# One weight load of 8 MB cut into four strided loads at the start of a streaming attention kernel

## The chip, the cores and the metric

The kernel runs on one core of a Trainium2 chip. The metric is the device time of one launch in microseconds (us). It was run three times for that: 1309.45, 1309.56 and 1309.97 us, with a median of 1309.56 us. One further execution was taken with the profiler. Its lines are those quoted below.

## The reference

Four tokens `x` (4 x 512) go through two branches whose outputs are mixed by a gate.

```
q = (x @ wq) as 32 heads of 128             # wq: 512 x 4096 f32, 8 MB
scores = q . k_cache / sqrt(128)            # k_cache: 4 x 32 x 4096 x 128 f32, 256 MB
a = softmax(scores) . v_cache @ wo          # v_cache: the same size; wo: 4096 x 512
b = (gelu(x @ w_gate) * (x @ w_up)) @ w_down   # 512 x 1792 twice, 1792 x 512
g = sigmoid(sum(x * gate_w))
out = g * a + (1 - g) * b
```

Every byte of the two caches is read once, and little is computed with each. Of the 565 MB that are read, `wq` is 8 MB.

## The kernel before

**Tiling.** The caches are cut into 32 tiles each, one for a token (4) and a group of four heads (8). A tile is 8 MB: 128 partitions with 64 KB each. One large SBUF buffer, `big`, holds two K tiles, which overlap by a quarter, and one V tile. Before the first K tile has been used, the place of the V tile holds `wq`.

**Order.** The kernel records its steps in a `Plan`. Each step has an engine, a lane (a semaphore of its own) and the ranges that it reads and writes; the plan works out from these who waits for whom. `play` then emits the steps: the waits, the instruction, and an increment of the lane's semaphore by the lane's unit, which is 16 for a load. All loads are issued from one queue, that of SyncE (SP), in the order in which they are recorded: `load` records one, `load_kv` a tile of a cache, `load_f`, `load_d` and `load_w` the other weights.

**The start.** The opening steps are played inside a critical section, which the other engines leave after SP has issued them. They are four loads: `wq` (lane `q`), `x` (lane `x`, 4 rows of 2 KB), `gate_w` (lane `g`, sent to 4 partitions) and the first K tile (lane `k`). `wq` is viewed as 128 rows of 64 KB, one for each partition: partition p holds four rows of the weight matrix. Then the constants and masks are made, `x` is transposed (L307), `q_project` (L325) multiplies it by `wq` in 64 short matmuls, and VectorE puts the result in the form that all later tiles use. `load_f` reuses the place of `wq`, so its loads wait for `q_project`.

**The steady part.** For each tile VectorE multiplies K by q (L379) and sums over the head dimension (L385), ScalarE takes the exponential, and TensorE multiplies by V (L411). The next K tile is loaded once the shared quarter of the present one is done with, and the next V tile once TensorE is done with the last. At the end `w_down` and `wo` follow, and the output of 8 KB is stored (L603).

In the text, a *mover* is one of the 16 DMA engines of the core, a *row* is the 64 KB of one partition, which a mover carries as one packet, and *landing* is the arrival of a transfer's last semaphore increment.

Of the kernel before, what the change touches and what calls it, by code (L numbers as in the profile page):

```python
# [19 lines left out]
class Plan:  # L20
# [18 lines left out]
    def add(self, engine, emit, reads=(), writes=(), lane=None, unit=1):  # L39
        lane = lane or engine  # L40
        self.units[lane] = unit
        row = self.by_lane.setdefault(lane, [])
        step = Step(lane, engine, emit, self.turn if engine in self.loops else None)
        step.at = len(row)
        need = {}
        for accesses, writing in ((reads, False), (writes, True)):
            for name, lo, hi in accesses:
                for other, a, b, wrote in self.past.get(name, ()):
                    if a < hi and lo < b and (wrote or writing):
                        if other.lane == engine and engine == "pe":  # L50
                            continue
                        if other.lane == engine and not wrote:
                            continue
                        need[other.lane] = max(need.get(other.lane, -1), other.at)
        seen = self.seen[engine]
        for l, n in sorted(need.items(), key=lambda x: -len(self.by_lane[x[0]])):
            if seen.get(l, -1) >= n:
                continue
            other = self.by_lane[l][n]
            other.asked = True  # L60
            step.waits[l] = n
            seen[l] = n
            for k, v in self.knew[other].items():
                seen[k] = max(seen.get(k, -1), v)
        step.waits = {l: n for l, n in step.waits.items()
                      if not any(self.knew[self.by_lane[m][k]].get(l, -1) >= n for m, k in step.waits.items() if m != l)}
        self.knew[step] = dict(seen)
        self.knew[step][lane] = step.at
        if row and lane == engine:
            for k, v in self.knew[row[-1]].items():  # L70
                if k != lane:
                    self.knew[step][k] = max(self.knew[step].get(k, -1), v)
        for accesses, writing in ((reads, False), (writes, True)):
            for name, lo, hi in accesses:
                old = self.past.get(name, [])
                if writing:
                    old = [x for x in old if not (lo <= x[1] and x[2] <= hi)]
                self.past[name] = old + [(step, lo, hi, writing)]
        row.append(step)
        self.steps.append(step)  # L80
        return step
# [14 lines left out]
    def wants(self, step):  # L96
        return {l: self.by_lane[l][n].value for l, n in step.waits.items()}

    def play(self, steps, wants=None):
        for s in steps:  # L100
            e = self.engines[s.engine]
            for l, v in sorted((wants(s) if wants else self.wants(s)).items()):
                e.wait_ge(self.sems[l], v)
            last = s.emit()
            if s.asked:
                last.then_inc(self.sems[s.lane], self.units[s.lane])

    def loop(self, engine):
        steps = [s for s in self.steps if s.engine == engine and s.turn is not None]
# [23 lines left out]
def tile_gated_mix(tc: tile.TileContext, x, kc, vc, wq, wo, w_gate, w_up, w_down, gate_w, out):  # L133
    nc = tc.nc
    P = 128
    B, H, S, D = kc.shape
    DM = x.shape[2]
    F = w_gate.shape[1]
    KC = DM // P
# [27 lines left out]
    def sb(pool, name, shape):  # L167
        sizes[name] = math.prod(shape[1:])
        return pool(name, [P] + list(shape[1:]), F32).ap()[:shape[0]]
# [37 lines left out]
    q = sb(ps, "q", [P, B, D])  # L207
# [6 lines left out]
    Q0, F0, F1, W0, D0 = VA, VA, VA + KC * F, VA, VA + TW // 2  # L214
# [4 lines left out]
    def place(a, n):  # L219
        return big[:, a:a + n]  # L220

    def z(a, n):
        return ("big", a, a + n)
# [14 lines left out]
    plan = Plan(nc)  # L238
    add = plan.add
# [14 lines left out]
    def load(dst, src, writes, lane):  # L254
        return add("sp", lambda: nc.sync.dma_start(dst, src), (), writes, lane=lane, unit=16)  # L255
# [28 lines left out]
            else:  # L284
                load(place(a, m), src[:, e0 * DM:e1 * DM], [z(a, m)], lane)

    load(place(Q0, KC * H * D), wq.rearrange("(p c) n -> p (c n)", c=KC), [z(Q0, KC * H * D)], "q")
    load(x_sb, x.rearrange("b s d -> (b s) d"), [z(XS, DM)], "x")
    load(gw, gate_w.rearrange("(s n) -> s n", s=1).to_broadcast([B, DM]), [z(GS, DM)], "g")
    load_kv("k", 0)  # L290
# [187 lines left out]
    def attended(w, e):  # L478
        a, m = ES + w * E * 32 + e * 32, (W0, W1)[w] + e * DM
        return place(a, 32), place(m, DM), [z(a, 32), z(m, DM)]  # L480
# [112 lines left out]
    s, w, reads = attended(1, E - 1)  # L593
    for h in range(2):
        lo = reads[1][1] + h * DM // 2
        project(s, w, [reads[0], z(lo, DM // 2)], False, True, (2 * h, 2 * h + 1))
        for c, move in ((2 * h + 1, act), (2 * h, dve)):
            dst, read, write = res[:B, c * C4:(c + 1) * C4], [(("acc", "po0")[h], 0, C4)], [("res", c * C4, (c + 1) * C4)]
# [46 lines left out]
```

## Time and profile before

| what | value |
|---|---|
| median of three runs | 1309.56 us |
| the profiled execution's own time | 1309.54 us |
| span of its instructions | 1308.2 us |
| DMA queue 1 | 10968 packets, 564.69 MB, busy 99.7% of the span |
| bytes per time over the span | 432 GB/s |
| VectorE busy | 1155.2 us (88%) |
| TensorE busy | 355.4 us (27%) |
| ScalarE busy | 87.4 us (7%) |

The span is the time from the first to the last instruction; the execution's own time is 1.3 us longer. The DMA share is the mean over the 16 movers, and a window counts a packet, with its whole duration and all its bytes, where it starts. So a window that is shorter than a packet shows a share above 1 or below it. The product of a window's share, its length and 16 is the summed duration of the packets that started in it, and its GB/s times its length is their size. In this way one packet can be read by a window that is only as wide as its start.

### The profile page before, as it was taken

The numbers are of one execution on the slowest core, as the hardware profiler recorded it, in microseconds if no ns is written. First come the engines' busy times: TensorE is split into PE (matmuls) and PEld (weight loads), VectorE is DVE, ScalarE is ACT, GpSimd is POOL, SyncE is SP. The second block draws the span as 40 slices with busy tenths as digits, with TensorE's granted clock in tenths as the row PEclk, the third lists the DMA queues.
The fourth block names the chain that finished last, engine by engine and source line by source line (L and its number), as shares of the span: only waits on it lengthen the run. The fifth ranks groups of instructions, "written<-read, shape, count | busy, mean of one in ns | idle before, by whom it ended". The sixth has DMA issues, their size and how long they took to land.

```text
span 1308.2 us, 6148 instructions
## 1 busy us (share of the span) xinstructions
PE 355.4 (27%) x2504; PEld 100.7 (8%) x2504; DVE 1155.2 (88%) x299; ACT 87.4 (7%) x291; POOL 0.7 (0%) x6
## 2 busy tenths in 40 slices
PE   2402233212332211322321223331133222122327
PEld 0100001000010000100000000100001000010003
DVE  1899999999899998989989898998989899898991
ACT  0000000000000000000000000000000000000001
POOL 0000000000000000000000000000000000000000
PEclk9656666556676656666655666655566665666668
DMA  9999999999999999999999999999999999999998
GB/s 417 419 445 421 445 419 445 429 437 439 431 439 427 439 427 443 423 445 429 437 437 431 439 429 439 427 441 425 443 425 443 435 433 439 429 439 427 439 428 369
DMA packets 10977, 564.81 MB, mean 432 GB/s; under 512 B 1228, under 2 KB 1484, under 8 KB 1880
## 3 DMA queue, kind: packets, MB, share of 16 engines
q1 hardware_dynamic: 10968, 564.69, 99.7%
q8 instruction: 6, 0.10, 0.0%
q14 instruction: 3, 0.02, 0.0%
HBM read 564.67 MB, written 0.01 MB: 432 GB/s over the span
## 4 chain that ended last, share of the span: by engine, by line
DMA 72%; DVE 26%; PE 1%; issue 1%; SPq 0%; ACT 0%; DVEq 0%; POOLq 0%
DMA big<-in_A_k_cache 66%; DVE sc L385 13%; DVE big L379 12%; DMA big<-in_A_wo 2%; DMA big<-in_B_w_up 2%; DMA big<-in_A_x 2%; PE po L325 1%; PE q L506 0%; PE acc L493 0%; SPq L255 0%; PE wide L485 0%; DVE hT L525 0%; DVE m L390 0%; DVE xT L312 0%; DVE big L523 0%
## 5 line engine op out<-in xcount | busy, mean ns | idle before, releaser
L379 DVE TENSOR_TENSOR big<-big,qb 128x4096 f32<-128x4096 f32 x64 | 555.9, 8687 | 87.8 <-DMA big<-in_A_k_cache 87.8
L385 DVE TENSOR_REDUCE sc<-big 128x32 f32<-128x4096 f32 x64 | 555.9, 8686 | 2.3
L411 PE MATMUL po<-big,PM 128*32 128x512 f32 x2048 | 296.0, 743 | 899.9 <-DMA big<-in_A_v_cache 899.9
L411 PEld LDWEIGHTS po<-big,PM 128*32 128x32 f32 x2048 | 72.8, 133 | 1116.9 <-DMA big<-in_A_v_cache 824.7
L397 ACT ACTIVATE PM<-sc,nb 32x128 f32<-32x128 f32 x128 | 67.2, 525 | 478.0 <-DVE nb L392 431.3
L419 ACT ACTIVATE o<-po 128x512 f32<-128x512 f32 x16 | 9.6, 597 | 448.5 <-PE po L411 448.5
L397 ACT ACTIVATION_READ_ACCUMULATOR PM<-sc,nb 32x1 f32 x128 | 26.1, 204 | 0.0
L369 ACT ACTIVATE qb<-q 128x512 f32<-128x512 f32 x8 | 4.8, 597 | 246.9 <-PE q L367 246.9
L428 PE MATMUL sm<-o,sel 128*16 128x128 f32 x128 | 15.4, 273 | 5.1 <-ACT o L419 5.1
L312 DVE COPY xT<-sg 128x128 f32<-128x128 f32 x4 | 0.9, 282 | 17.9 <-PE sg L307 17.9
L506 PE MATMUL q<-big,xT 128*32 128x448 f32 x64 | 10.9, 853 | 15.4 <-DMA big<-in_B_w_gate 11.3
L461 DVE TENSOR_TENSOR tm<-oT,gmask 128x256 f32<-128x256 f32 x2 | 0.8, 425 | 13.8 <-PE oT L455 13.8
L428 PEld LDWEIGHTS sm<-o,sel 128*16 128x16 f32 x128 | 11.7, 97 | 12.8 <-ACT o L419 11.4
L602 DVE COPY res<-acc 4x128 f32<-4x128 f32 x1 | 0.3, 278 | 11.9 <-PE acc L493 11.9
L367 PE MATMUL q<-QM,hc 128*128 128x512 f32 x16 | 9.5, 678 | 4.2 <-DVE hc L363 4.2
L390 DVE TENSOR_REDUCE m<-sc 128x1 f32<-128x128 f32 x32 | 9.2, 286 | 1.1
L325 PE MATMUL po<-big,xT 128*32 128x512 f32 x64 | 8.5, 693 | 1.0 <-DVE xT L312 1.0
L391 DVE STREAM_TRANSPOSE mt<-m 128x32 f32<-128x32 f32 x32 | 6.8, 211 | 1.1
L485 PE MATMUL wide<-big 128*32 128x512 f32 x54 | 6.6, 597 | 1.2 <-DMA big<-in_A_wo 1.2
L392 DVE TENSOR_REDUCE nb<-mt 128x1 f32<-128x32 f32 x32 | 6.0, 186 | 1.1
L307 PE MATMUL sg<-ident,big 4*128 4x4 f32 x4 | 0.6, 254 | 23.2 <-DMA big<-in_A_x 23.2
L342 DVE TENSOR_TENSOR big<-po,amask 128x512 f32<-128x512 f32 x2 | 1.3, 686 | 5.8 <-PE po L325 5.8
(72 smaller groups left out, 58.6 us busy)
## 6 DMA issues: line engine op xcount, KB each, us to landing
big<-in_A_wo SPq DMA_DIRECT2D x1, 4096.0 KB, 27.5
big<-in_B_w_gate SPq DMA_DIRECT2D x1, 3584.0 KB, 17.4
big<-in_B_w_up SPq DMA_DIRECT2D x1, 3584.0 KB, 26.4
big<-in_B_w_down SPq DMA_DIRECT2D x1, 3584.0 KB, 18.2
big<-in_A_wo SPq DMA_DIRECT2D x2, 1024.0 KB, 25.4
big<-in_A_wo SPq DMA_DIRECT2D x2, 768.0 KB, 29.1
big<-in_A_k_cache SPq DMA_DIRECT2D x32, 29.7
big<-in_A_v_cache SPq DMA_DIRECT2D x32, 29.3
```

Source lines behind the costliest of these rows:

```text
L325: last = T.matmul(PO[s][32 * j:32 * j + 32].rearrange("p j d -> p (j d)"), xTf[:, c, :32], w[:, n0:n0 + HB * D], start=c == 0, stop=c == K ...
L367: pe(lambda: T.matmul(q.rearrange("p b d -> p (b d)"), HC.rearrange("p h k -> p (h k)"), QM.rearrange("p b d -> p (b d)"), start=True, sto ...
L379: dve(lambda: V.tensor_tensor(k, k, QB[:, b:b + 1, :].to_broadcast([P, r1 - r0, D]), op=OP.mult), m + t("qb"), m)
L385: dve(lambda: V.tensor_reduce(SC[i % 2][:, r0:r1], k, axis=AX.X, op=OP.add), [z(KA(i) + r0 * D, (r1 - r0) * D)], [(f"sc{i % 2}", r0, r1)])
L390: dve(lambda: V.tensor_reduce(M1[n], SC[n], axis=AX.X, op=OP.max), t(f"sc{n}"), t(f"m1{n}"))
L391: dve(lambda: V.transpose(MT, M1[n].to_broadcast([P, PH])), t(f"m1{n}"), t("mt"))
L397: last = A.activation(PM[:, PZ:].rearrange("p (c m) -> p c m", m=32)[s, :, h:RJ * HT:HT], SC[n][s, :].rearrange("p (c j) -> p c j", j=RJ), ...
L411: last = T.matmul(PO[n][32 * c:32 * c + 32].rearrange("p j d -> p (j d)"), PM[:, m0:m0 + 32], place(VAT(i) + j * N, N), start=b == 0 and j ...
L419: act(lambda: A.activation(O[n], PO[n], AF.Copy), t(f"po{n}"), t(f"o{n}"))
L428: T.matmul(sm[:B * HT, :D], selv[:, j, m0:m0 + B * HT], O[n][:, j, :], start=(n, j) == (0, 0), stop=(n, j) == (N - 1, RJ - 1))
L485: pe(lambda: T.matmul(wide[32 * c:32 * c + 32, :], s, w, start=n < 4, stop=n >= NW - 4), reads, t("wide"))
L506: last = T.matmul(q.rearrange("p b d -> p (b d)")[32 * j:32 * j + 32, :FG], xTf[:, c, :32], place((F0, F1)[s] + c * F + j * FG, FG), start ...
```

## The change

The load of `wq` becomes a step that issues four loads. They take the partitions 0, 8, 16, ... (16 rows), 1, 3, 5, ... (64 rows), 2, 6, 10, ... (32 rows) and 4, 12, 20, ... (16 rows), in this order; together they are the same 128 rows. All four increase the semaphore of a new lane `wq` by 16 each, and `q_project` waits for 64. Lane `q` is left to the load of the first half of `wo`, which used it too.

```diff
             if s.asked:
-                last.then_inc(self.sems[s.lane], self.units[s.lane])
+                last.then_inc(self.sems[s.lane], min(self.units[s.lane], 16))
...
-    load(place(Q0, KC * H * D), wq.rearrange("(p c) n -> p (c n)", c=KC), [z(Q0, KC * H * D)], "q")
+    def load_wq():
+        dst, src = place(Q0, KC * H * D), wq.rearrange("(p c) n -> p (c n)", c=KC)
+        steps = ((0, 8), (1, 2), (2, 4), (4, 8))
+        for i, (p, n) in enumerate(steps):
+            last = nc.sync.dma_start(dst[p::n], src[p::n])
+            if i < len(steps) - 1:
+                last.then_inc(plan.sems["wq"], 16)
+        return last
+
+    add("sp", load_wq, (), [z(Q0, KC * H * D)], lane="wq", unit=64)
```

The change moves rows on one queue only. SP's list begins so before (each row is an instruction, `128x16384` its partitions and elements):

```order
L641 UNCONDITIONAL_BRANCH
L612 UNCONDITIONAL_BRANCH
L255 DMA big<-in_A_wq 128x16384
L255 DMA big<-in_A_x 4x512
L255 DMA big<-in_gate_w 4x512
L255 DMA big<-in_A_k_cache 128x16384
```

With the change, at the same place of the same queue, it begins so:

```order
L650 UNCONDITIONAL_BRANCH
L621 UNCONDITIONAL_BRANCH
L291 DMA big<-in_A_wq 16x16384
L291 DMA big<-in_A_wq 64x16384
L291 DMA big<-in_A_wq 32x16384
L291 DMA big<-in_A_wq 16x16384
L255 DMA big<-in_A_x 4x512
L255 DMA big<-in_gate_w 4x512
L255 DMA big<-in_A_k_cache 128x16384
```

The loads of `x`, `gate_w` and the first K tile stand three issues later; the instructions of the other engines keep their order.

## The prediction

> **What bounds the kernel now.** I read the page first: its slices, the queues, and the time that the packets took.
>
> ```profile
> DVE  1899999999899998989989898998989899898991
> DMA  9999999999999999999999999999999999999998
> q1 hardware_dynamic: 10968, 564.69, 99.7%
> ```
>
> VectorE has gaps, the movers have none. The windows (length, then the five engines, granted clock, DMA share, GB/s) say the same of single stages, the first two of which are `wq` and the first K tile:
>
> ```profile
> 1.90:21.78 19.88, 0.00 (x0) 0.00 (x0) 1.76 (x8) 1.28 (x1) 0.50 (x2) 1.00 1.01 422
> 21.78:41.13 19.35, 11.26 (x72) 3.46 (x72) 7.68 (x19) 0.69 (x2) 0.00 (x0) 0.92 1.00 434
> 600.00:700.00 100.00, 30.44 (x212) 8.62 (x212) 90.85 (x23) 8.11 (x27) 0.00 (x0) 0.65 1.00 433
> 1200.00:1300.00 100.00, 40.88 (x307) 13.89 (x310) 75.91 (x27) 6.77 (x21) 0.00 (x0) 0.65 0.99 429
> ```
>
> The share is 0.99 to 1.01 throughout. So from 1.90 us on the movers always have a row to carry, and the time is a start, then 565 MB at the movers' own pace, then a short tail. Whatever `wq` costs the movers more or less shifts all that follows, and nothing catches it up. The chain of waits begins with a load that is late for the same reason (start, length):
>
> ```profile
> 1.33 21.71 DMA big<-in_A_x
> ```
>
> `x` is queued behind `wq` on the same movers, and lands at 1.33 + 21.71 = 23.04 us. The next load that must wait for the projection is `w_gate`. SP's own timeline shows what is issued when (start, length):
>
> ```profile
> 0.89 0.39 SPq L255 DMA_DIRECT2D big<-in_A_wq  x1
> 1.33 0.36 SPq L255 DMA_DIRECT2D big<-in_A_x  x1
> 1.75 0.26 SPq L255 DMA_DIRECT2D big<-in_gate_w  x1
> 2.05 0.36 SPq L255 DMA_DIRECT2D big<-in_A_k_cache  x1
> 33.35 0.35 SPq L255 DMA_DIRECT2D big<-in_B_w_gate  x1
> ```
>
> `w_gate` is issued at 33.35 us, and the rows of the first K tile keep the movers busy to 41.13 us: 7.8 us to spare. When `wq` lands later by some time, the K tile lands later by the same, so that this cover moves along and isn't used up.
>
> **The change part by part.** *Three more issues.* Issues on SP start 0.30 to 0.44 us apart above, so the K tile's issue goes from 2.05 to about 3.3 us. It is needed when the movers have carried `wq`, at 21.78 us: hidden by 18 us. The second load must be there when the first one's row is done, at least 2.4 us after it began, and follows after 0.44 us: hidden. The other engines leave the critical section about 1.3 us later:
>
> ```profile
> 3.42 0.20 POOL L293 MEMSET ident<- 128x128 f32 x1 [2.98 <-POOLq L612]
> 5.85 0.07 DVE L303 MEMSET RS<- 128x16 f32 x1
> 23.18 0.61 PE L307 MATMUL sg<-ident,big 4*128 4x4 f32 x4 [23.18 <-DMA big<-in_A_x]
> ```
>
> Their constants are done at 5.92 us, would be done at 7.2, and are used at 23.18: hidden. Without this cover it would be 1.3 us. The wait of `q_project` for 64 in place of 16 costs nothing, since `x` comes behind the same rows.
>
> *A quicker first row.* These windows hold the starts of the first 16 rows, of the second 16, the time after the issue of the final store of 4 rows, and its packets:
>
> ```profile
> 1.90:2.66 0.76, 0.00 (x0) 0.00 (x0) 0.00 (x0) 0.00 (x0) 0.00 (x0) 1.00 4.12 1380
> 4.86:5.52 0.66, 0.00 (x0) 0.00 (x0) 0.55 (x1) 0.00 (x0) 0.00 (x0) 1.00 3.67 1589
> 1306.70:1307.50 0.80, 0.00 (x0) 0.00 (x0) 0.00 (x0) 0.00 (x0) 0.00 (x0) 1.00 0.00 0
> 1307.50:1307.90 0.40, 0.00 (x0) 0.00 (x0) 0.00 (x0) 0.00 (x0) 0.00 (x0) 1.00 0.07 21
> ...
> 1306.77 0.29 SPq L603 DMA_DIRECT2D out<-res  x1
> ```
>
> The first rows took 4.12 x 0.76 x 16 / 16 = 3.13 us each, the second ones 3.67 x 0.66 = 2.42. That is 0.71 us lost while the first load starts. And its first packet comes 1.90 - 0.89 = 1.01 us after the issue, that of the store of four rows 1307.50 - 1306.77 = 0.73 us after, or 0.28 us sooner. If a load of 16 rows starts like the store and its row runs at full pace, 0.71 + 0.28 = 1.0 us is won; if neither depends on the number of rows, nothing. The bounds are 0 and -1.0; I take -0.5, since the row nearest in kind (the store) is a small one and supports only the smaller part.
>
> *The pace of the rows.* Each mover carries 8 rows of `wq` before and after (128 / 16; and 1 + 4 + 2 + 1). At 2.42 us each that is 19.36 us, as the K tile's 19.35 shows. The unknown is whether a mover keeps this pace when the rows of one load are not 128 neighbouring partitions. The trace has one load of another shape, `x` with `gate_w`: both go to partitions 0 to 3, eight packets of 2 KB. These windows show six of them and the first K row of two movers:
>
> ```profile
> 22.01:22.02 0.01, 0.00 (x0) 0.00 (x0) 0.00 (x0) 0.00 (x0) 0.00 (x0) 1.00 16.33 6554
> 22.07:22.09 0.02, 0.00 (x0) 0.00 (x0) 0.00 (x0) 0.00 (x0) 0.00 (x0) 1.00 0.55 205
> 22.15:22.17 0.02, 0.00 (x0) 0.00 (x0) 0.00 (x0) 0.00 (x0) 0.00 (x0) 1.00 0.58 205
> 22.42:22.43 0.01, 0.00 (x0) 0.00 (x0) 0.00 (x0) 0.00 (x0) 0.00 (x0) 1.00 0.53 205
> 22.50:22.51 0.01, 0.00 (x0) 0.00 (x0) 0.00 (x0) 0.00 (x0) 0.00 (x0) 1.00 0.58 205
> 22.59:22.60 0.01, 0.00 (x0) 0.00 (x0) 0.00 (x0) 0.00 (x0) 0.00 (x0) 1.00 15.11 6554
> ```
>
> 205 GB/s for 0.02 us is two packets of 2 KB, for 0.01 us one, and 6554 GB/s for 0.01 us is one row. The packet of 22.42 took 0.53 x 0.01 x 16 = 0.085 us. The K row that began at 22.01, while six such packets of other movers were still to come, took 16.33 x 0.01 x 16 = 2.61 us; the one that began at 22.59, after all of them, 15.11 x 0.01 x 16 = 2.42. So movers that write into neighbouring partitions seem to hinder each other: 0.19 us lost beside 6 x 0.085 = 0.51 us of foreign packets, or 0.37 of what it would be if only one of them could write at a time. In the full loads of 128 partitions none is hindered.
>
> Of the four new loads, the two with 16 rows put one row on each mover and touch every eighth partition. If a way into the SBUF serves partitions in groups of four, as the packets into 0 to 3 suggest, they use half of the groups, and two movers can meet on one way. At worst each then waits for the other and a row takes 2 x 2.42 us. The bounds for a mover: nothing in any row; 2.42 us more in each of its 8 rows, 19.36 us. Between these lie: full price in the two sparse loads, 2 x 2.42 = 4.84 us; the price of the hindered K row (0.37) in those two, 1.8 us; the same in all eight, 7.2 us. I take 4.84, the full price where the spacing is widest; it is also near the middle of the two sums by the hindered row.
>
> [...]
>
> **The sum.** The profiled execution's 1309.54 us (1308.2 of span and 1.3 around it) is within 0.02 of the median, 1309.56. From the median: - 0.5 (start) + 4.84 (rows) + 0 (issues, waits) gives 1313.9 us. With 1.8 to 7.2 us for the rows the forecast's own range is 1310.9 to 1316.8.
>
> **The rivals.** *No hindrance at all.* The 2 KB packets themselves kept their 0.085 us side by side (22.07 has two at once at 0.55 x 0.02 x 16 / 2 = 0.088), and a single late row can have another cause. Then only the quicker start is left: 1309.56 - 0.5 = 1309.1 us, between 1308.6 and 1309.6. It comes to the same if the loads of 16 rows do not do what their shape says: should they fall to fewer movers, the other movers go on with the next load, and each has its 8 rows in the end. *Hindered in every row.* If a load's rows are dealt out in their order, movers meet in the loads of 64 and 32 rows as well, at full price: 1309.56 - 0.5 + 19.36 = 1328.4 us. For it speaks that none of the four loads has the shape that runs free; against it the mild 0.37. *Faster by more than 0.2%* (2.6 us, about what a measurement of this kernel can tell from no change): all that the start can give is the 1.0 us above, and the movers have no other gap; it would need a better pace than 2.42 us, which no window shows.
>
> **How the numbers follow.** Forecast 0.38 (of which 0.02 lies under 2.6 us), no hindrance 0.33, hindered in every row 0.25, faster 0.03, a time between the forecast and the full price 0.01. So slower is 0.36 + 0.25 + 0.01 = 0.62, the same 0.33 + 0.02 = 0.35, faster 0.03. The range must reach from the rival without hindrance to the one with all of it, 1308.6 to 1328.4, and over it by the start's 0.5 us, should that not be won: 1308.6 to 1329.0.
>
> **What would show it.** Right: the windows of `wq` show about 4.8 us more between the first packet and the first K row, with rows of near 4.8 us in the first and the last of the four loads and 2.42 in the others, and the K tile's landing and all later issues shift by as much. Wrong, to the rival without hindrance: all rows at 2.42 us and the K rows beginning before 21.8 us. Wrong, to full price: rows near 4.8 us all through `wq` and the K rows beginning near 41 us. Wrong as a whole if the rows keep their pace and the end still moves by over 2.6 us, for then the movers would have had a gap elsewhere. The first row's duration against 3.13 us settles the term of the start, and the constants' end before `x` lands that of the issues.

## The result and the profile after

The changed kernel took 1314.95 us (median of 6 runs, 1314.61 to 1315.53) against 1309.51 us for the kernel before (6 runs, 1309.04 to 1309.97): 5.4 us more. The ratio is 1.0042, with a 95% interval of 1.0029 to 1.0055. The span of the profiled execution grew from 1308.2 to 1313.9 us.

The page of the changed kernel has the lines that were shown of before:

```profile
DVE  1699999999999999999999989999899998998991
DMA  9999999999999999999999999999999999999998
q1 hardware_dynamic: 11016, 564.69, 99.7%
```

The movers are as full as before, and the bytes are the same; the 48 further packets (11016 against 10968) are 16 for each of the three further loads. On SP's timeline (start, length) the four issues stand as one line:

```profile
0.90 2.60 SPq L291 DMA_DIRECT2D big<-in_A_wq  x4
3.54 0.52 SPq L255 DMA_DIRECT2D big<-in_A_x  x1
4.11 0.26 SPq L255 DMA_DIRECT2D big<-in_gate_w  x1
4.41 0.36 SPq L255 DMA_DIRECT2D big<-in_A_k_cache  x1
38.69 0.35 SPq L255 DMA_DIRECT2D big<-in_B_w_gate  x1
```

`w_gate` is issued at 38.69 us, before at 33.35: 5.3 us later. So the loss is already complete when `wq` has been used. The windows of the changed kernel show where it lies. After the first, each holds the starts of 16 rows, as many as there are movers (GB/s times length is 1.05 MB), so that share times length is the mean duration of a row; the last but one holds the eight small packets of `x` and `gate_w` as well:

```profile
0.90:2.30 1.40, 0.00 (x0) 0.00 (x0) 0.00 (x0) 0.00 (x0) 0.00 (x0) 1.00 0.00 0
2.30:3.45 1.15, 0.00 (x0) 0.00 (x0) 0.00 (x0) 0.00 (x0) 0.00 (x0) 1.00 4.14 912
6.86:7.97 1.11, 0.00 (x0) 0.00 (x0) 0.94 (x4) 0.21 (x1) 0.00 (x0) 1.00 2.69 945
12.40:13.25 0.85, 0.00 (x0) 0.00 (x0) 0.00 (x0) 0.00 (x0) 0.00 (x0) 1.00 2.85 1234
17.30:18.04 0.74, 0.00 (x0) 0.00 (x0) 0.00 (x0) 0.00 (x0) 0.00 (x0) 1.00 3.28 1417
22.13:23.14 1.01, 0.00 (x0) 0.00 (x0) 0.00 (x0) 0.00 (x0) 0.00 (x0) 1.00 4.76 1038
26.67:28.10 1.43, 0.00 (x0) 0.00 (x0) 0.00 (x0) 0.00 (x0) 0.00 (x0) 1.00 2.11 745
29.87:30.90 1.03, 0.81 (x4) 0.20 (x8) 1.00 (x3) 0.00 (x0) 0.00 (x0) 1.00 2.35 1018
```

The first line has no packet: the first one starts at 2.30 us, not at 1.90. The rows of the first load (every eighth partition) took 4.14 x 1.15 = 4.76 us. The first rows of the second load took 2.69 x 1.11 = 2.99; they begin between 6.86 and 7.97 us, while other movers are still in the first load. Then come rows of 2.85 x 0.85 = 2.42 us (odd partitions) and 3.28 x 0.74 = 2.43 (every fourth). The rows of the last load took 4.76 x 1.01 = 4.81 us, the first K rows, with the small packets counted in, 2.11 x 1.43 = 3.02, or about 2.9 without them, and the second K rows again 2.35 x 1.03 = 2.42. These begin at 29.87 us. Before, the same rows began at 24.20, as this window of the kernel before shows:

```profile
24.20:25.02 0.82, 0.26 (x4) 0.20 (x8) 0.82 (x4) 0.00 (x0) 0.00 (x0) 1.00 2.95 1279
```

That is 5.7 us, the whole difference of the two spans. Later issues stay late by about as much: the next two K tiles are issued at 57.15 and 98.85 us, before at 51.31 and 93.38.

### The profile page after: what moved, and what is told of

Read it like the earlier page. It is cut to its first block, busy times and chain, and to the rows that moved or that the text cites. A ratio compares the mean times of both kernels' runs of the same rounds, so it can differ in the third digit from the quotient of the medians.

```text
span 1313.9 us, 6151 instructions
## 1 busy us (share of the span) xinstructions
PE 355.4 (27%) x2504; PEld 100.9 (8%) x2504; DVE 1155.3 (88%) x299; ACT 87.4 (7%) x291; POOL 0.7 (0%) x6
## 3 DMA queue, kind: packets, MB, share of 16 engines
q1 hardware_dynamic: 11016, 564.69, 99.7%
## 4 chain that ended last, share of the span: by engine, by line
DMA 72%; DVE 26%; PE 1%; issue 1%; SPq 0%; ACT 0%; DVEq 0%; POOLq 0%
DMA big<-in_A_k_cache 65%; DVE sc L394 13%; DVE big L388 12%; DMA big<-in_A_wo 2%; DMA big<-in_B_w_up 2%; DMA big<-in_A_x 2%; PE po L334 1%; PE q L515 0%; SPq L291 0%; PE acc L502 0%; PE wide L494 0%; DVE hT L534 0%; DVE xT L321 0%; DVE m L399 0%; SPq L255 0%
```

## The experiments

My theory, an estimate from the K row that took 2.61 in place of 2.42 us: two movers share a way into the SBUF when a load leaves out whole groups of partitions, and a load of every eighth partition leaves out half of them. It has two rivals. By the first, each further load, or a load with one row for each mover, costs a fixed time. By the second, the rows are slow on the memory side, because they are read 512 KB apart. Each experiment changes only how `load_wq` cuts the load, and with it the number that `q_project` waits for (16 for each load).

**Two loads, the even and the odd partitions.**

```diff
-        steps = ((0, 8), (1, 2), (2, 4), (4, 8))
+        steps = ((0, 2), (1, 2))
```

> wq in two loads of 64 rows, the even partitions and then the odd ones. Shared ways into the SBUF (two movers meet only where a load leaves out whole groups of four partitions): every group is reached, so rows stay at 2.42 us and the time is that of before plus the later first packet (0.4 us) at most: 1309.4 to 1310.1 us. Cost per load (each load beyond the first costs the movers a fixed time; three of them cost 5.4 us in the changed kernel, so 1.8 us each): 1311.3 us. Strided source rows (the memory side is slow when rows are read at a distance): rows slower than 2.42 us in both loads, 1311 us or more.

Measured: 1309.78 us (10 runs), ratio 1.0001 (0.9991 to 1.0010).

**Two loads, partitions 0 to 63 and 64 to 127.**

```diff
-        steps = ((0, 8), (1, 2), (2, 4), (4, 8))
-        for i, (p, n) in enumerate(steps):
-            last = nc.sync.dma_start(dst[p::n], src[p::n])
+        n = 64
+        for p in range(0, P, n):
+            last = nc.sync.dma_start(dst[p:p + n], src[p:p + n])
```

> wq in two loads of 64 rows, partitions 0 to 63 and then 64 to 127: as many loads, rows and bytes per mover as with the even and the odd partitions, but each load leaves out half of the groups of four. Shared ways: two movers on each way throughout, rows of 4.84 us, 8 rows per mover, 19.4 us more: 1329 us. Cost per load: 1311.3 us, as with alternate partitions. Strided source rows: the source is one block per load, so 1309.5 us.

Measured: 1330.55 us (4 runs), ratio 1.0161 (1.0144 to 1.0178). These two kernels have the same number of loads, rows and bytes per mover, and lie 20.8 us apart. A window with 16 rows of each, the alternate partitions first and then the halves:

```profile
12.50:13.10 0.60, 0.00 (x0) 0.00 (x0) 0.00 (x0) 0.00 (x0) 0.00 (x0) 1.00 4.05 1748
```

```profile
11.70:13.10 1.40, 0.00 (x0) 0.00 (x0) 0.00 (x0) 0.00 (x0) 0.00 (x0) 1.00 3.66 749
```

4.05 x 0.60 = 2.43 us a row against 3.66 x 1.40 = 5.12. Which partitions a load touches decides between these two; how many loads there are does not. A strided source as such does not make rows slow here: the halves read one block each and are slow, the alternate rows are read 128 KB apart and run free. Rows read 512 KB apart are tested two experiments below. The 1329 us expected took 4.84 us a row, so it was 1.5 us low.

**Four loads, each every fourth partition.**

```diff
-        steps = ((0, 8), (1, 2), (2, 4), (4, 8))
+        steps = ((0, 4), (1, 4), (2, 4), (3, 4))
```

> wq in four loads of 32 rows, each every fourth partition. As many loads as in the changed kernel, none with only one row for each mover. Shared ways: each load reaches every group of four once, so rows stay at 2.42 us; only the later first packet is left: 1309.4 to 1310.2 us. Cost per load: three further loads as in the change, 1315 us. Strided source rows: between, 1311 to 1315 us.

Measured: 1309.72 us (10 runs), ratio 1.0003 (0.9993 to 1.0012). Four loads in place of one cost nothing that these runs can tell. A window of it has rows of 3.03 x 0.80 = 2.42 us:

```profile
12.40:13.20 0.80, 0.00 (x0) 0.00 (x0) 0.00 (x0) 0.00 (x0) 0.00 (x0) 1.00 3.03 1311
```

**The changed kernel's partitions, with the source read in blocks.** The projection then uses the rows of `wq` in another order than the reference, so this kernel's output is not the reference's.

```diff
-        steps = ((0, 8), (1, 2), (2, 4), (4, 8))
-        for i, (p, n) in enumerate(steps):
-            last = nc.sync.dma_start(dst[p::n], src[p::n])
+        steps = ((0, 8, 0), (1, 2, 16), (2, 4, 80), (4, 8, 112))
+        for i, (p, n, r) in enumerate(steps):
+            last = nc.sync.dma_start(dst[p::n], src[r:r + P // n])
```

> The changed kernel's four loads into the same partitions, but each reads its rows as one block of wq (rows 0 to 15, 16 to 79, 80 to 111, 112 to 127), so the projection uses rows in another order. Shared ways: what counts is where the rows go, so the same as the changed kernel, 1315 us with rows near 4.8 us in the first and last load. Cost per load: the same, 1315 us. Strided source rows: the loss is gone, 1309.5 to 1310 us.

Measured: 1314.50 us (5 runs), ratio 1.0037 (1.0023 to 1.0052), as the changed kernel. The rows of its last load, whose source is now one block of 1 MB, are as slow as there, 7.86 x 0.60 = 4.72 us:

```profile
22.10:22.70 0.60, 0.00 (x0) 0.00 (x0) 0.00 (x0) 0.00 (x0) 0.00 (x0) 1.00 7.86 1748
```

So it is the destination, not the distance at which the source is read.

**Eight loads of 16 rows, every eighth partition.** The size of the effect, and whether it needs the beginning or the end of the stream:

```diff
-        steps = ((0, 8), (1, 2), (2, 4), (4, 8))
+        steps = tuple((i, 8) for i in range(8))
```

> wq in eight loads of 16 rows, each every eighth partition. Shared ways: all eight rows of a mover are carried at the pace that the two halves showed (5.13 us a row), so 8 x 5.13 = 41.0 us for wq in place of 19.4 and 0.4 us for the later first packet: near 1331.5 us. Loss only where a sparse load begins or ends the stream (first and last load of the change): 1315 us.

Measured: 1330.67 us (2 runs), ratio 1.0161 (1.0141 to 1.0181). The loss isn't tied to the first or the last load. By this run alone a fixed price for each load of 16 rows would do as well: the changed kernel has two of them for 5.4 us, so eight would cost 21.6, and 21.1 us were measured. The halves, which cost as much and have no load of 16 rows, speak against it, and so do the next loads.

**Eight loads of 16 neighbouring partitions.**

```diff
-        steps = ((0, 8), (1, 2), (2, 4), (4, 8))
-        for i, (p, n) in enumerate(steps):
-            last = nc.sync.dma_start(dst[p::n], src[p::n])
+        n = 16
+        for p in range(0, P, n):
+            last = nc.sync.dma_start(dst[p:p + n], src[p:p + n])
```

> wq in eight loads of 16 neighbouring partitions (0 to 15, 16 to 31 and so on): as many loads, rows and bytes as in eight loads of every eighth partition. Shared ways by groups of four partitions: each load reaches four groups, four movers on each way, rows of about 4 x 2.42 to 4 x 2.57 = 9.7 to 10.3 us, 77 to 82 us for wq: 1367 to 1373 us. If a way served a whole half of the SBUF instead (partitions 0 to 63 and 64 to 127 at half the rate each): the same as the two halves, 1330.5 us. Loss by number of loads: the same as the eight strided loads.

Measured: 1388.06 us in the profiled execution and 1364.51 us in the other. In the profiled one the rows of `wq` took 9.3 us each, but the cache rows behind them were slow, too. Its page shows this in 40 slices of 34.7 us, here above the same line of a second pair of executions, described below:

```profile
GB/s 121 121 309 388 394 391 390 389 396 431 444 427 429 444 427 429 444 429 431 442 431 437 433 431 442 427 431 444 427 429 444 427 429 444 429 431 441 433 433 369
GB/s 123 123 327 441 431 433 431 433 439 442 431 433 433 431 437 431 433 439 440 433 433 433 431 435 433 431 440 440 433 431 433 433 433 435 431 435 441 435 431 368
```

The 390 GB/s of the slices from 104 to 312 us are 2.7 us a row for 16 movers; after that the pace is that of the other kernels. So it was a stretch of some 200 us and not, as the next expectation has it, all cache rows. What caused it the runs do not show. The second pair:

> The eight loads of 16 neighbouring partitions once more, since the profiled execution of the first time had all its cache rows at 2.7 us in place of 2.42. Shared ways by groups of four partitions: rows of wq again near 9.3 us, four movers on each way, and with cache rows at 2.42 us a time near the 1364.5 us of the other execution. A way for each half of the SBUF: 1330.5 us.

Measured: 1364.11 us (2 runs, 1364.08 and 1364.14), ratio 1.0410 (1.0380 to 1.0441).

**Four loads of 32 neighbouring partitions.**

```diff
-        steps = ((0, 8), (1, 2), (2, 4), (4, 8))
-        for i, (p, n) in enumerate(steps):
-            last = nc.sync.dma_start(dst[p::n], src[p::n])
+        n = 32
+        for p in range(0, P, n):
+            last = nc.sync.dma_start(dst[p:p + n], src[p:p + n])
```

> wq in four loads of 32 neighbouring partitions. [...] Shared ways, where each group of four has a way of its own and 64 neighbours are slow for another reason: 32 neighbours reach half as many, so rows twice as long as in the two halves, about 1371 us.

Measured: 1330.08 us (2 runs), ratio 1.0156 (1.0136 to 1.0177). A window with 16 rows of each of the three, first of every eighth partition:

```profile
11.80:13.10 1.30, 0.00 (x0) 0.00 (x0) 0.00 (x0) 0.00 (x0) 0.00 (x0) 1.00 3.95 807
```

of 16 neighbours (the second pair of executions):

```profile
36.80:39.40 2.60, 0.00 (x0) 0.00 (x0) 0.00 (x0) 0.00 (x0) 0.00 (x0) 1.00 3.59 403
```

and of 32 neighbours:

```profile
11.50:12.50 1.00, 0.00 (x0) 0.00 (x0) 0.00 (x0) 0.00 (x0) 0.00 (x0) 1.00 5.14 1049
```

A row took 3.95 x 1.30 = 5.14 us, 3.59 x 2.60 = 9.33 us and 5.14 x 1.00 = 5.14 us. The first and the second have equal numbers of loads and rows, and cost 21.1 and 54.0 us; so no fixed price for a load of 16 rows explains them. The second's rows are near four times 2.42 us, as if four movers shared a way. A way for each half of the SBUF, for which 1330.5 us were expected, does not fit the 1364.11. The third ran like the halves, with rows of 5.14 against 5.12 us and 1330.08 against 1330.55 us: 64 neighbours are served no faster than 32, and the 1371 us that rows of twice the length would have taken did not come. Why 64 are no faster is not shown: the traces do not tell which mover carries which partition. My expectation for 16 neighbours was too high at both ends (1367 to 1373 us for 1364), since a row cost less than 4 x 2.42 us.

**Two loads of all partitions, cut along the rows.** The first load takes the first eighth of each row, the second the rest. This was to settle the later first packet, and it is the one cut that might have beaten both kernels.

```diff
-        steps = ((0, 8), (1, 2), (2, 4), (4, 8))
-        for i, (p, n) in enumerate(steps):
-            last = nc.sync.dma_start(dst[p::n], src[p::n])
+        cuts = (0, KC * H * D // 8, KC * H * D)
+        for lo, hi in zip(cuts, cuts[1:]):
+            last = nc.sync.dma_start(dst[:, lo:hi], src[:, lo:hi])
```

> wq in two loads of all 128 partitions: the first eighth of each row (8 KB) and then the other seven eighths. No part of the partitions is left out. Shared ways: no hindrance; and the first packet starts as early as before, near 1.9 us, if the later start of the other splits comes from loads of fewer than 128 partitions: 1309.5 us within 0.3. If the later start comes from having several loads in the place of one, the first packet comes near 2.2 us: 1309.8 us. If the 0.7 us that the first packets lose depend on their size, up to 0.6 us less: 1308.9 us.

Measured: 1309.49 us (10 runs), ratio 1.0000 (0.9990 to 1.0009): no version here is faster than the kernel before. The timelines of SP's first issue, and a window of the first packets, for this kernel:

```profile
0.89 0.39 SPq L291 DMA_DIRECT2D big<-in_A_wq  x1
...
1.90:2.50 0.60, 0.00 (x0) 0.00 (x0) 0.00 (x0) 0.00 (x0) 0.00 (x0) 1.00 1.24 218
2.66:3.01 0.35, 0.00 (x0) 0.00 (x0) 0.00 (x0) 0.00 (x0) 0.00 (x0) 1.00 0.86 351
```

for the alternate partitions:

```profile
0.89 0.56 SPq L291 DMA_DIRECT2D big<-in_A_wq  x1
...
1.90:2.20 0.30, 0.00 (x0) 0.00 (x0) 0.00 (x0) 0.00 (x0) 0.00 (x0) 1.00 0.00 0
2.20:3.20 1.00, 0.00 (x0) 0.00 (x0) 0.00 (x0) 0.00 (x0) 0.00 (x0) 1.00 3.06 1049
```

and for 32 neighbours:

```profile
0.89 0.39 SPq L291 DMA_DIRECT2D big<-in_A_wq  x1
...
1.90:2.20 0.30, 0.00 (x0) 0.00 (x0) 0.00 (x0) 0.00 (x0) 0.00 (x0) 1.00 16.18 3495
```

The first packet comes about 1.0 us after the start of an issue that takes 0.39 us, and 1.3 us after the start of one that takes 0.56. So in these runs the later start follows the length of the first issue, not the number of loads: there are four in the last kernel, two in the one above it. Small first packets start slowly too (1.24 x 0.60 = 0.74 us each; then the 15 of the second window, 123 KB, 0.86 x 0.35 x 16 / 15 = 0.32 us), which is 0.4 us lost in place of the 0.7 of whole rows, and the time is the same as far as the runs can tell. So the larger part of the loss at the start isn't a matter of size. Fewer rows do not shorten it either: the alternate partitions' first rows took 3.06 us. In the changed kernel, whose four issues take 2.60 us together, 0.63 the first, the first packet comes 1.4 us after the start of the first.

## Why the prediction was right, and where it was not

**Direction and mechanism.** It forecast 1313.9 us by hindered rows in the two loads of 16 rows and free ones in the others. The rows of 4.76 and 4.81 us in the first and the last load, and of 2.42 and 2.43 between, are that case and no other. That the movers have no gap, so that what is lost on `wq` is lost at the end, held too: 5.7 us at the second K rows and 5.7 us in the span.

**The rows (+4.84).** Measured: the first two rows of a mover took 4.76 + 2.99 us, before 3.13 + 2.42, so 2.2 more. The last row of `wq` and the next one, at 4.81 and about 2.9 in place of 2.42 each, cost 2.9 more. Together 5.1. The term was right within 0.3 us, but in part by luck. The two hindered rows cost only 1.6 + 2.4 = 4.0 us more, not 4.84, since the first row was slow before as well. And the row behind each of them, which I had put at 2.42 us, cost 0.6 and 0.5 us more: the hindrance did not end with the load. I put that down to movers that were done and began the next row (from 6.86 us on) while others were still in the sparse load. These two errors nearly cancel. Of my two reasons for the full price, the spacing of the partitions held. The other, that it lies "near the middle of the two sums by the hindered row", was no support, for that row's price of 0.37 came from packets of 2 KB, and the runs show no such discount for whole rows: in eight loads of every eighth partition a row takes 5.14 us, 2.1 times 2.42. Why the short packets cost so little wasn't tried.

**The start (-0.5).** This is the term that failed, outside both of its bounds (0 and -1.0): the first packet came at 2.30 in place of 1.90 us, 0.4 us later. I compared with the final store of four rows, but the load of 16 strided rows is not issued like it (0.63 us against 0.29); the part that was to be won from the slow first row wasn't there, since first rows take 3.06 us with the alternate partitions as well; in the first rows of 4.76 us it can't be told from the hindrance. The sum is 0.4 + 5.1 = 5.5 us, against 5.4 measured and 5.7 between the two profiled spans; the errors of the two terms (0.9 and 0.3) account for the 1.05 us by which the forecast was low.

**The issues and waits (0).** Right. The K tile's issue moved to 4.41 us, later than my 3.3, because each of the four issues takes 0.57 to 0.67 us and not 0.4, and that of `x` 0.52 and not 0.36; the cover of 18 us swallows that. The constants end at 8.28 us, not at the 7.2 expected, and `x` lands at 3.54 + 24.82 = 28.36:

```profile
8.21 0.07 DVE L312 MEMSET RS<- 128x16 f32 x1
```

**The ranges.** Two bounds were not worked out alike. The forecast's 1310.9 has the start's -0.5 us in it and its 1316.8 has not; with it, it is 1316.3. And the full price without the start's gain is 1309.56 + 19.36 = 1328.9 us, not 1329.0. Neither changes the account.

**The rivals.** No hindrance fell in the changed kernel itself, by its rows of 4.76 and 4.81 us, and again with the halves and the eight loads. Hindered in every row fell there too; its premise, that movers also meet in the loads of 64 and 32 rows, is refuted by the alternate partitions and by every fourth one, both free, with rows of 2.43 and 2.42 us. What the movers share, and by which groups of partitions, no trace shows; groups of four were my estimate from the packets into partitions 0 to 3. What the traces show is the rate of 16 rows of 64 KB: 2.42 us or 433 GB/s for every fourth partition, 5.14 us or 204 GB/s for every eighth one and for 32 neighbours, 5.12 us or 205 GB/s for 64, and 9.33 us or 112 GB/s for 16.

## What to carry to other kernels

When a kernel's movers are never idle, judge a cut of a load by the partitions that each piece touches: pieces that keep every second or every fourth partition cost nothing here that the runs can tell (2.43 and 2.42 us a row), while every eighth one, or a block of 64 or 32 neighbours, ran at slightly under half the rate (5.12 to 5.14 us) and a block of 16 at about a quarter (9.33 us). The stall of 0.19 us on one packet beside small ones pointed to this loss, but its size was no price for whole rows, which lost up to 2.7 us each in loads of every eighth partition. And the number of loads, or the issue time, told little here, where the issues were covered by a full queue: four loads of every fourth partition took 1309.72 us, and the K tile's issue came 2.4 us later in the changed kernel (4.41 for 2.05) under a cover of 18 us.

## What was not expected of the hardware

Loads of every eighth partition and of 32 neighbours fell below half of the pace: 5.14 us a row, not 2 x 2.42 = 4.84. Those of 16 neighbours took 9.33, less than 4 x 2.42 = 9.68. The length of the first issue differed with the shape of the load: 0.39 us for 128 or 32 neighbouring partitions, 0.56 for every second one, and 0.57 for 64 neighbours on the timeline of the halves. What sets it stays open.

```profile
0.89 0.57 SPq L291 DMA_DIRECT2D big<-in_A_wq  x1
```
